# A convolution and an expert network on one core: block 1's convolution one slot later, block 2's input asked for earlier

## The chip, the core and the metric

The kernel runs on one core of a Trainium2 chip. A core has five engines with queues of their own: TensorE (PE in the profile, its weight loads PEld), VectorE (DVE), ScalarE (ACT), GpSimd (POOL) and SyncE (SP), which here only issues transfers. The engines meet at semaphores: an instruction adds to one when it ends, another engine waits until it has reached a value. The metric is the device time of one execution in microseconds (us); smaller is better.

## What is computed

The input x has 8 sequences of 4096 tokens with 192 features each. A causal convolution with 7 taps mixes each token with the six before it; its weights are a softmax over the taps, one set for each of 8 groups of 24 features. Its result goes through W_in (192 x 2048), an exact GELU, and W_out (2048 x 192).

```python
w = softmax(weight)                          # (8 heads, 7 taps)
x_pad = concatenate([zeros(B, 6, D), x], axis=1)
conv[b, s, h, g] = sum_k w[h, k] * x_pad[b, s + k, 24 * h + g]
h = conv.reshape(B * S, 192) @ w_in          # 32768 x 2048
g = 0.5 * h * (1.0 + erf(h / sqrt(2)))
out = g @ w_out                              # 32768 x 192
```

## The kernel before

**Tiling.** The 32768 tokens are two halves of 16384, which sit in the two halves of the 128 partitions. A *block* is a run of tokens taken from both halves at once: blocks 0 to 5 have 256 tokens of each half, all later ones 512 (`WS`, L33). The 192 features are three groups of 64 (`p`), the 2048 hidden features 16 chunks of 128.

**Stages of a block.** SyncE loads x (`load`, L326, four transfers for a block). VectorE transposes it (`trans`, L473) so that features lie on partitions. The convolution follows. From block 2 on, VectorE does it tap by tap (`conv`, L498). For blocks 0 and 1, at the start, TensorE does it, with diagonal matrices of tap weights (`pconv`, L669): first another engine casts the transposed x to bf16 (`cast`, L219; for block 1 that is GpSimd), then TensorE sums the taps into a PSUM bank, and then VectorE (for block 0 also ScalarE) casts the sum to `xc` (`conv_out`, L188). A block has four such sums (`kinds`, L171), called kd 0 to 3; the last two are half as wide. One `pconv` call is a pair of matmuls, one for each half of the tokens.

**Slots and units.** TensorE then runs a block as *slots*. A slot is one call of `mm1` (L706): it multiplies `xc` by some of W_in's columns into one of two PSUM tiles `hp`, and ScalarE takes that tile through GELU into `gT` (L653). With two tiles, slot u waits until the gelu of slot u - 2 has ended (L710). A block of 256 tokens has 8 slots. Between the slots TensorE runs the second product, gT times W_out, of the block before: one call of `mm2` (L749) is a *unit* of two matmuls. A small block has 64 units: two groups of tokens, each with two passes (`ph`) over 16 chunks. In block 0, and in block 1, the units behind the slots are both of block 0's product, since there is none earlier: the first 12 run behind block 0's last slots, the other 52 behind block 1's. The list `ws` (L834) says behind which slots. Block 0's units 0, 4, 8 and 12 each wait for one of W_out's four transfers (`S_WOUT`, L839), and unit 4j of the first group waits for the gelus whose outputs it reads (L765). Unit 16, the first of the second pass, waits for the end of the first pass (L760).

The dictionary `behind` (L704) places block 1's `pconv` pairs behind slots of block 0: `p01` is the 14 pairs of kd 0 and 1, `p2` the 14 half-wide pairs of kd 2 and 3. A convolution pair uses TensorE in tiles of 64 rows by 64 columns. `mm1` uses 64 by 128, but in those of block 0's slots that have convolution pairs behind them and before the next slot it uses twice as many matmuls of 64 by 64 (`fw`, L735).

**W_in in both halves.** Each token half needs W_in on its own partitions. GpSimd loads each column group once, into one half, with six transfers: two counted by `S_WIN[0]` and `S_WIN[1]`, two by `S_WIN[2]`, and two larger ones by `S_WIN[3]` and `S_WIN[4]`. VectorE copies each to the other half (`dup`, L465; six copies, counted by `S_DUPE`). Slots 1, 3, 4 and 6 of block 0 wait for 2, 4, 5 and 6 of these copies (L720).

**Orders written out by hand.** VectorE's order at the start is L545 to L562: among others the copies 3 and 4 (`dup(1, 0)`, `dup(1, 1)`), block 1's last transposition, copy 5, three evictions of block 1 (kd 0 and both halves of kd 1), copy 6 (`dup(2, 1)`), three more evictions, and then block 2's transposition and its convolution. GpSimd's is L424 to L434: the fifth W_in transfer, a wait for the second, the sixth W_in transfer, two W_out transfers, a cast, another cast and a W_out transfer, a third cast and the last W_out transfer. SyncE's is L850 to L861: x of blocks 0 and 1, then a wait, x of block 2, a wait for W_out's last transfer, x of block 3, and from there loads and stores in turn.

Of the kernel before, what the change touches and what calls it, by code (L numbers as in the profile page):

```python
# [11 lines left out]
def bass_lightweight_conv__then__act_gelu_exact_kernel(  # L12
# [54 lines left out]
    NSL = [NF // c for c in NCH]  # L67
# [5 lines left out]
    M0, M1 = 6, NB - 1  # L73

    PHC, MMC, EVC = [0], [0], [0]
    for n in range(NB):
        new = M0 <= n < M1
# [25 lines left out]
    def sem(name):  # L103
        return es.enter_context(nc.semaphore(name))

    def ap(t, off, pat):
        return bass.AP(t, off, pat)

    with es:
# [24 lines left out]
        S_WIN = [sem("S_WIN%d" % i) for i in range(5)]  # L134
        S_WOUT = [sem("S_WOUT%d" % i) for i in range(4)]
# [66 lines left out]
        def wait_pc(e, n, p):  # L202

            if n == 0:
                e.wait_ge(S_PCA, p + 1)
                if p >= 1:
                    e.wait_ge(S_PCE, p)
            else:
                e.wait_ge(S_PCE, len(PV) + (1, 3, 6)[p])
# [23 lines left out]
        def cvd(n):  # L233

            return sum(NCV - 2 * (m in K0) for m in range(n + 1) if m not in PC)
# [58 lines left out]
        def store_half(e, g, h):  # L294
            m = NB - 1
            if h == 0:
                wait_ev(e, m, g)
            else:
                e.wait_ge(S_EVB, g + 1)
            e.dma_start(  # L300
                ap(outt, (h * HALF + OFF[m] + 128 * g) * C, [[C, 128], [1, C]]),
                osb[m % 2][:, (4 * h + g) * C : (4 * h + g + 1) * C],
            ).then_inc(S_OUT[m % 2], 16)
# [22 lines left out]
        def load(e, n, qs=(0, 2, 1, 3), sm=None):  # L326
            mb = WS[n] // 32
            if n >= NX:
                e.wait_ge(S_TR, trd(n - NX))
            for q in qs:  # L330
                off = ((q // 2) * HALF + OFF[n]) * D + DQ * (q % 2)
                dst = [[TB // 32 * DQ, 32], [DQ, mb], [1, DQ]]
                src = [[D, 32], [32 * D, mb], [1, DQ]]
                e.dma_start(
                    ap(xin[n % NX], 32 * q * (TB // 32 * DQ), dst), ap(xt, off, src)
                ).then_inc(sm or S_XIN[n % NX], 16)
# [327 lines left out]
        def _(t):  # L664
# [4 lines left out]
            def pconv(n, kd, k):  # L669

                p, ex, c0, w = kinds(n)[kd]
                if k == KS - 1:
                    t.wait_ge(S_CAST[PC[n]], p + 1)
                    if n == 0:
                        t.wait_ge(S_DG, 1)
                if n == 0 and k == 2:
                    t.wait_ge(S_DGA, 3)
                if k == KS - 2:
                    t.wait_ge(S_HALO, n + 1)
                for hf in range(2):  # L680
                    ho = hf ^ ex
                    r = slice(64 * hf, 64 * hf + 64)
                    d0 = k * 64
                    x0 = p * XB + HF + k + c0
                    ins = t.matmul(  # L685
                        bank(kd, slice(64 * ho, 64 * ho + 64), w),
                        dg[r, d0 : d0 + 64],
                        xTb[PC[n]][r, x0 : x0 + w],
                        start=(k == KS - 1),
                        stop=(k == 0),  # L690
                        tile_position=(64 * hf, 64 * ho),
                    )
                if k == 0:
                    ins.then_inc(S_PC)
# [6 lines left out]

            p01 = [(1, kd, k) for k in taps for kd in (0, 1)]
            p2 = [(1, kd, k) for k in taps for kd in (2, 3)]
            behind = {(0, 2): p01[:8], (0, 3): p01[8:] + p2[:2], (0, 4): p2[2:]}  # L704

            def mm1(n, i):  # L706
                w, c = WS[n], NCH[n]
                u = SL0[n] + i
                if u >= 2:
                    t.wait_ge(S_GELU, u - 1)  # L710
                if i == 0:
                    if n in PC:
                        wait_pc(t, n, NP - 2)
                    else:
                        t.wait_ge(S_CV, cvd(n) - 1)
                if n == 0:
                    for j, k in {0: ((0, 16), (1, 16)), 2: ((2, 32),), 4: ((3, 16),), 6: ((4, 16),)}.get(i, ()):
                        t.wait_ge(S_WIN[j], k)
                    if i in (1, 3, 4, 6):
                        t.wait_ge(S_DUPE, (0, 2, 0, 4, 5, 0, 6)[i])  # L720
                todo = [(cc, p) for cc in range(c) for p in range(NP)]
                head = (n, i) == (0, 0)
                if head:
                    todo.sort(key=lambda q: q[1] == NP - 1)
                for cc, p in todo:
                    if i == 0 and cc == 0 and p == NP - 1:
                        if n in PC:
                            wait_pc(t, n, p)
                        else:
                            t.wait_ge(S_CV, cvd(n))  # L730
                    for hf in range(2):
                        r = slice(64 * hf, 64 * hf + 64)
                        ch = CH[hf][i * c + cc]
                        f0 = FQ * ((ch // 2) ^ hf) + ch % 2
                        fw = 64 if (n == 0 and 3 <= i <= 4) or M0 < n <= M1 else 128  # L735
                        for fo in range(0, 128, fw):
                            f1 = 64 * hf * NP * F + p * F + f0 + 2 * fo
                            o = hf * TB + cc * w
                            ins = t.matmul(  # L739
                                hp[u % 2][fo : fo + fw, o : o + w],  # L740
                                ap(win, f1, [[NP * F, 64], [2, fw]]),
                                xc[n % 2][r, p * TB : p * TB + w],
                                start=(p == 0 and (cc == 0 or not head)),
                                stop=(p == NP - 1 and (cc == c - 1 or not head)),
                                tile_position=(64 * hf, fo),
                            )
                ins.then_inc(S_MM1)
# [68 lines left out]
            SHARE = [3, 3, 3, 3, 4, 3, 3, 3, 3, 4, 3, 3, 3, 3, 2, 2]  # L816

            def units(m):
                if M0 <= m < M1:
                    return [(ps, i) for ps in range(3) for i in range(NF)]  # L820
                return [
                    (g, ph, i) for g in range(NG[m]) for ph in range(2) for i in range(NF)
                ]

            for n in range(NB):
                todo = units(max(n - 1, 0))
                if n < 2:
                    todo = todo[12:] if n else todo[:12]
                for i in range(NSL[n]):
                    mm1(n, i)  # L830
                    for q in behind.get((n, i), []):
                        pconv(*q)
                    new = M0 < n <= M1
                    ws = SHARE if new else [0] * 5 + [1] * 3 if n == 0 else [1] * NSL[n]  # L834
                    a0 = len(todo) * sum(ws[:i]) // sum(ws)
                    a1 = len(todo) * sum(ws[: i + 1]) // sum(ws)
                    for un in todo[a0:a1]:
                        if n < 2 and un[:2] == (0, 0) and un[2] % 4 == 0:
                            t.wait_ge(S_WOUT[un[2] // 4], 16)  # L839
                        (mm2_t if new else mm2)(max(n - 1, 0), *un)  # L840
# [7 lines left out]
        @block.sync  # L848
        def _(sp):
            sp.dma_start(wsb[:, :], ap(wt, 0, [[KS, H], [1, KS]])).then_inc(S_WSB, 16)  # L850
            load(sp, 0, (0, 1))

            sp.wait_ge(S_PRO, 2)
            load(sp, 1)
            sp.wait_ge(S_WOUT[0], 16)
            load(sp, 2)
            sp.wait_ge(S_WOUT[3], 16)
            load(sp, 3)
            for n in range(1, NB):
                if n + 3 < NB:  # L860
                    load(sp, n + 3)  # L861
                store(sp, n - 1)
            for g in range(NG[NB - 1]):
                store_half(sp, g, 0)
            for s in range(2):
                sp.wait_ge(S_OUT[s], OUTS[NB - 1 if (NB - 1) % 2 == s else NB - 2])
# [28 lines left out]
```

## Time and profile before

| what | value |
|---|---|
| median of 4 runs | 680.98 us (680.86 to 681.99) |
| the profiled execution | 680.86 us |
| its span, first to last instruction | 679.1 us |
| granted TensorE clock | 1.000 |
| gelus (L653) | 512, mean 1024 ns |
| mm1 matmuls (L739) | 6072, mean 365 ns |
| block 1's evictions on VectorE begin | 12.97 us |
| VectorE's transposition of block 2 begins | 18.73 us |

Times inside the span are counted from its first instruction. The profiled execution's time is 1.8 us longer than its span, by what lies around the instructions. An engine's busy time is the union of its instructions' times; TensorE's matmuls overlap, so a matmul's duration (0.27 us for 256 columns) is not what it costs, and the distance between starts is. "Idle before" names the semaphore that came last before an instruction.

### The profile page before, as it was taken

What the parts mean: (1) busy time and instruction counts of PE and PEld (TensorE: products, weight loads), DVE (VectorE), ACT (ScalarE), POOL (GpSimd) and SP (SyncE); (2) the same over time, 40 slices, a digit from 0 to 9 for tenths busy, and PEclk for the clock granted to TensorE, in tenths of its full rate; (3) what the DMA queues carried; (4) which work ended last, traced back from release to release, by engine and by line L of the source; (5) the groups of instructions that cost most, each with busy time, mean ns of one, the idle gap of its engine ahead of it and who ended that gap; (6) DMA issues with size and microseconds to landing.
All of it is one profiled execution on the core that took longest, in us unless ns stands there. A gap on an engine that the chain in (4) does not pass through costs nothing.

```text
span 679.1 us, 27122 instructions
## 1 busy us (share of the span) xinstructions
PE 674.2 (99%) x12632; PEld 411.8 (61%) x12632; DVE 527.4 (78%) x609; ACT 537.2 (79%) x550; POOL 32.7 (5%) x56
## 2 busy tenths in 40 slices
PE   8999999999999999999999999999999999999998
PEld 8899655555555555555555555555555555555557
DVE  6889978977779877779777788777797777887511
ACT  7899977787778777787877777877877777778772
POOL 5010000000000000000000000000000000000000
PEclk9999999999999999999999999999999999999999
DMA  9435324224443234442244432244422444310223
GB/s 153 107 95 131 70 61 94 52 50 93 95 96 78 47 68 96 95 96 58 46 90 95 96 76 51 65 96 95 97 57 50 85 96 95 89 37 21 49 49 96
DMA packets 134177, 53.66 MB, mean 79 GB/s; under 512 B 127408, under 2 KB 134064, under 8 KB 134064
## 3 DMA queue, kind: packets, MB, share of 16 engines
q1 hardware_dynamic: 130224, 49.76, 32.6%
q0 software_dynamic: 2720, 1.57, 1.8%
q8 instruction: 99, 1.62, 1.0%
q10 hardware_dynamic: 1120, 0.59, 0.3%
q14 instruction: 14, 0.11, 0.1%
HBM read 28.31 MB, written 25.17 MB: 79 GB/s over the span
## 4 chain that ended last, share of the span: by engine, by line
PE 97%; DMA 1%; POOL 1%; ACT 0%; issue 0%; DVE 0%
PE hp L739 48%; PE ob L800 43%; PE ob L771 5%; PE hp L771 1%; DMA win<-in_moe_w_in_dram 1%; ACT gT L653 0%; POOL wout L404 0%; POOL win L371 0%; DMA wsb<-in_weight_dram 0%; PE ob L685 0%; POOL xTb L226 0%; DVE osb L290 0%
## 5 line engine op out<-in xcount | busy, mean ns | idle before, releaser
L653 ACT ACTIVATE gT<-hp 128x1024 bf16<-128x1024 f32 x512 | 523.3, 1024 | 128.3 <-PE hp L739 124.6
L739 PE MATMUL hp<-xc,win 64*64 64x512 bf16 (+2 forms) x6072 | 418.7, 365 | 0.8 <-ACT gT L653 0.5
L800 PE MATMUL ob<-gT,wout 64*64 64x512 bf16 x5376 | 366.3, 376 | 0.0
L524 DVE SCALAR_TENSOR_TENSOR acc<-xT,wcol,acc 128x1024 f32<-128x1024 f32 (+1 forms) x330 | 295.3, 945 | 3.0 <-ACT acc L626 2.9
L739 PEld LDWEIGHTS hp<-xc,win 64*64 64x64 bf16 (+1 forms) x6072 | 188.5, 106 | 133.6 <-ACT gT L653 0.9
L800 PEld LDWEIGHTS ob<-gT,wout 64*64 64x64 bf16 x5376 | 172.3, 118 | 122.8
L321 DVE STREAM_TRANSPOSE osb<-ob 128x512 f32<-128x512 f32 x84 | 74.4, 888 | 128.9 <-PE ob L800 128.9
L496 DVE STREAM_TRANSPOSE xT<-xin 128x1536 f32<-128x1536 f32 (+2 forms) x39 | 74.9, 1925 | 3.5 <-DMA xin<-in_x_dram 3.4
L524 DVE SCALAR_TENSOR_TENSOR xc<-xT,wcol,acc 128x1024 bf16<-128x1024 f32 (+1 forms) x66 | 60.6, 959 | 0.0
L771 PE MATMUL ob<-wout,gT 64*128 64x192 bf16 x896 | 47.7, 243 | 0.3 <-ACT gT L653 0.2
L422 POOL COPY xT<-xT 128x18 f32<-128x18 f32 x30 | 22.6, 752 | 513.4 <-DVE xT L496 490.7
L771 PEld LDWEIGHTS ob<-wout,gT 64*128 64x128 bf16 x896 | 38.6, 94 | 6.2 <-PE ob L771 0.6
L517 DVE TENSOR_SCALAR acc<-xT,wcol 128x512 f32<-128x512 f32 (+2 forms) x60 | 33.7, 604 | 1.1
L292 ACT ACTIVATE osb<-ob 128x192 f32<-128x192 f32 x2 | 0.7, 332 | 7.1 <-PE ob L771 7.1
L667 PE MATMUL hp<-const-bfloat16-1.0 128*128 128x128 bf16 x48 | 5.3, 313 | 0.8 <-PEq L880 0.8
L771 PE MATMUL hp<-wout,gT 64*128 64x192 bf16 x128 | 5.9, 243 | 0.0
L667 PEld LDWEIGHTS hp<-const-bfloat16-1.0 128*128 128x128 bf16 x48 | 5.0, 149 | 0.8 <-issue 0.8
L290 DVE COPY osb<-ob 128x192 f32<-128x192 f32 x2 | 0.7, 358 | 6.1 <-PE ob L771 6.1
L771 PEld LDWEIGHTS hp<-wout,gT 64*128 64x128 bf16 x128 | 5.3, 94 | 0.0
L626 ACT ACTIVATE acc<-xT,wcol 128x256 f32<-128x256 f32 (+1 forms) x9 | 5.2, 579 | 0.0
L277 ACT ACTIVATE osb<-ob 128x384 f32<-128x384 f32 x10 | 4.9, 485 | 0.0
L685 PE MATMUL ob<-xTb,dg 64*64 64x256 bf16 (+1 forms) x112 | 4.1, 251 | 0.1
(35 smaller groups left out, 30.4 us busy)
## 6 DMA issues: line engine op xcount, KB each, us to landing
out_dram<-osb SPq DMA_DIRECT2D x124, 192.0 KB, 3.2
xin<-in_x_dram SPq DMA_DIRECT2D x116, 192.0 KB, 4.0
xin<-in_x_dram SPq DMA_DIRECT2D x22, 96.0 KB, 2.8
wout<-in_moe_w_out_dram POOLq DMA_DIRECT2D x4, 192.0 KB, 4.8
win<-in_moe_w_in_dram POOLq DMA_DIRECT2D x4, 96.0 KB, 4.8
win<-in_moe_w_in_dram POOLq DMA_DIRECT2D x2, 192.0 KB, 4.4
out_dram<-osb ACTq DMA_DIRECT2D x4, 96.0 KB, 1.9
out_dram<-osb SPq DMA_DIRECT2D x4, 96.0 KB, 2.4
```

The costliest lines, as they stand in the source:

```text
L277: e.activation(out=dst, in_=src, func=AF.Copy).then_inc(S_EVA)
L321: v.transpose(ap(osb[m % 2], j, [[8 * C, 128], [C // 2, TB // 32], [NP, 32]]), bank(ring(m, j)),).then_inc(S_EV)
L422: g.tensor_copy(dst, src).then_inc(S_HALO)
L496: v.transpose(out, src).then_inc(S_TR)
L517: ins = v.tensor_scalar(a, src, wk, None, ALU.mult)
L524: ins = v.scalar_tensor_tensor(dst, src, wk, a, op0=ALU.mult, op1=ALU.add)
L626: a.activation(out=acc[n % 2][:, p * TB : p * TB + w], in_=ap(xT[n % 2], p * XW + HX, [[NP * XW, 128], [1, w]]), func=AF.Copy, scale=wcol[ ...
L653: a.activation(out=ap(gT[n % 2], i * c * 2 * w, dst), in_=ap(hp[u % 2], 0, src), func=AF.Gelu,).then_inc(S_GELU)
L667: t.matmul(hp[1][:, 0:128], one, one)
L739: ins = t.matmul(hp[u % 2][fo : fo + fw, o : o + w], ap(win, f1, [[NP * F, 64], [2, fw]]), xc[n % 2][r, p * TB : p * TB + w], start=(p == ...
L771: ins = t.matmul(bb[sub], gT[m % 2][r, c0 : c0 + 128], wout[r, CH[sub][i] * C : (CH[sub][i] + 1) * C], start=(ph == 0 and k == 0), stop=(p ...
L800: ins = t.matmul(bank(ring(m, j), slice(64 * h, 64 * h + 64), w), ap(wout, 64 * hf * NF * C + CH[h][i] * C + j, [[NF * C, 64], [NP, 64]],) ...
```

## The change

Three things change. Block 1's convolution pairs move from behind slots 2, 3 and 4 to behind slots 3, 4 and 5, in the same three portions, and the tile form of `mm1` follows them. Block 0's units behind its own slots become 8 instead of 12: four each behind slots 6 and 7, none behind slot 5; the other 56 go behind block 1's eight slots, seven each. And SyncE asks for block 2's x when the transfer counted by `S_WIN[3]` (the fifth of W_in, the first of the two larger ones) has landed, where it waited for W_out's first. No instruction is added or removed in sum.

```diff
-            behind = {(0, 2): p01[:8], (0, 3): p01[8:] + p2[:2], (0, 4): p2[2:]}
+            behind = {(0, 3): p01[:8], (0, 4): p01[8:] + p2[:2], (0, 5): p2[2:]}
...
-                        fw = 64 if (n == 0 and 3 <= i <= 4) or M0 < n <= M1 else 128
+                        fw = 64 if (n == 0 and 4 <= i <= 5) or M0 < n <= M1 else 128
...
                 if n < 2:
-                    todo = todo[12:] if n else todo[:12]
+                    todo = todo[8:] if n else todo[:8]
...
-                    ws = SHARE if new else [0] * 5 + [1] * 3 if n == 0 else [1] * NSL[n]
+                    ws = SHARE if new else [0] * 6 + [1] * 2 if n == 0 else [1] * NSL[n]
...
             load(sp, 1)
-            sp.wait_ge(S_WOUT[0], 16)
+            sp.wait_ge(S_WIN[3], 16)
             load(sp, 2)
```

## The prediction

> **What bounds the kernel now.** I read the page's busy times first, then its 40 slices, then the busy times of single stretches.
>
> ```profile
> PE 674.2 (99%) x12632; PEld 411.8 (61%) x12632; DVE 527.4 (78%) x609; ACT 537.2 (79%) x550; POOL 32.7 (5%) x56
> ...
> PE   8999999999999999999999999999999999999998
> ```
> ```profile
> 30.00:650.00 620.00, 620.00 (x11538) 367.52 (x11536) 501.97 (x553) 498.65 (x500) 22.05 (x30) 1.00 0.35 77
> ```
>
> In the stretches each engine has its busy us and, in brackets, its instructions; the last three columns are the clock, the DMA share and GB/s. TensorE (PE) is without a gap from 30 to 650 us. Matmuls overlap in the trace, so I also went through the starts of all matmuls: after 25 us two intervals alone exceed 0.26 us before the tail at 665 us. So the end is set by when TensorE becomes full, and by nothing later. Next, the start on a timeline: TensorE, then ScalarE (ACT), then VectorE (DVE); the columns are start, duration, what, and the idle time before it.
>
> ```profile
> 10.22 0.83 PE L739 MATMUL hp<-xc,win 64*128 64x256 bf16 x12 [0.46 <-ACT gT L653]
> 11.00 1.04 PE L685 MATMUL ob<-xTb,dg 64*64 64x256 bf16 x16
> 11.78 0.92 PE L739 MATMUL hp<-xc,win 64*64 64x256 bf16 x24
> ...
> 15.04 0.83 PE L739 MATMUL hp<-xc,win 64*128 64x256 bf16 x12
> ...
> 18.06 0.91 PE L771 MATMUL ob<-wout,gT 64*128 64x192 bf16 x12 [0.22 <-ACT gT L653]
> ```
> ```profile
> 12.75 6.16 ACT L653 ACTIVATE gT<-hp 128x1024 bf16<-128x1024 f32 x6 [0.63 <-PE hp L739]
> ```
> ```profile
> 12.97 1.33 DVE L200 CAST xc<-ob 128x256 bf16<-128x256 f32 x3 [0.59 <-PE ob L685]
> 14.34 0.56 DVE L469 COPY win<-win 64x1536 bf16<-64x1536 bf16 x1
> 14.81 0.92 DVE L200 CAST xc<-ob 128x128 bf16<-128x128 f32 x3
> 18.73 1.22 DVE L496 STREAM_TRANSPOSE xT<-xin 128x768 f32<-128x768 f32 x1 [3.00 <-DMA xin<-in_x_dram]
> ```
>
> The reader is to see three things. At 11.00 block 1's convolution stands in front of slot 3 and waits for GpSimd's casts, so ScalarE idles 0.63 us. At 17.66 TensorE has issued its last matmul of block 1's slot 0, and stands until 18.06 for the gelu of block 0's slot 7. And VectorE makes the last of its six copies of W_in (14.34) *between* two groups of block 1's evictions; slot 6 starts at 15.04, right behind that copy's end at 14.90. VectorE's 3.00 us before block 2's transposition is long, but is it on the path?
>
> **What the skill says.** Perfetto Trace Analysis, Identifying the Most-Contended Engine: busy time of matmuls is a poor measure of how full TensorE is. The trace agrees: 12 matmuls of a slot show 0.83 us but the next kind starts 0.65 us after the first. I price by starts. DMA: Bandwidth & Descriptors, Issuing engines are not separate DMA queues: transfers from SyncE and GpSimd run on the same 16 engines and interleave. The trace agrees: from 5.0 to 7.5 us GpSimd's queue took 74.0% and SyncE's 50.7% of them together. TensorEngine Tiling (Array Packing), Key Properties: a change of tiling mode drains the array. Here the change from 64*64 to 64*128 ahead of slot 5 cost some 0.09 us (13.915 free, 14.006 started).
>
> **Prices, from starts.** One mm1 slot 0.655 us, in either tile form. One mm2 unit (two matmuls) 0.0825, from eight units in 0.66. Four 64*64 convolution matmuls 0.109 at 256 columns, 0.057 at 128. A gelu is 1.024 and begins 0.87 after its slot's first matmul (15.04 to 15.91, 16.02 to 16.89). A VectorE copy's end to the matmul that needs it: 0.145 (14.892 to 15.038).
>
> **The convolution, one slot later.** Nothing changes up to slot 2 at 10.22, which has issued at 10.88. Slot 3 now follows at once. It needs gelu 1 (ends 11.08) and the fourth W_in copy (two copies, 1.11 us from 10.13, end 11.24), so it starts at 11.38; with the 0.055 lag that the casts show it would be 11.29. It takes the 64*128 form and slot 5 the 64*64 form: 12 matmuls fewer and 12 more at one price, zero. Slot 3 is issued at 12.04. Its gelu can start at 12.25, 0.5 earlier than before: this is the gain. The first eight convolution pairs then cost 0.44 and a mode change, 0.09 (0 to 0.09), to 12.57. The casts, ready at 11.36, are now hidden behind slot 3. Slot 4: 12.57 to 13.22. The other six pairs and two narrow ones: 0.33 + 0.06, to 13.61. Slot 5: to 14.27. Twelve narrow pairs: 0.34, to 14.61. Here TensorE is free.
>
> Slot 6, however, needs the sixth W_in copy, and VectorE does that only after three evictions of block 1, which wait for the first two convolution sums. Their last matmul is issued at 13.44 and ends 0.27 later, so VectorE starts at 13.76 instead of 12.97. Evictions and copy take what they took: 1.92 us from 12.97 to 14.89, so the copy ends at 15.68 and slot 6 starts at 15.82 (15.70 with the short lags). That is 0.78 later than 15.04, and TensorE stands for 1.2 us. VectorE's own slack, the 0.59 us that it idles before the evictions, is no cover: what comes late is the sum that it waits for.
>
> **The eight pairs.** Block 0's product has 64 units. Before, 12 went behind slots 5 to 7 and 6 behind block 1's slot 0: 18 when block 1's slot 1 starts at 18.80. From slot 6 to there: 15.04 to 18.80 is 3.76 = three slots 1.965 + 14 units 1.155 + 0.40 for the gelu of slot 7 + 0.24 for the turn from the 16th unit to the 17th, which waits for the sums of its own bank. After: 4 + 4 + 7 = 15 units. Three slots 1.965 + 15 units 1.24 + 0.08 for the gelu (with the units moved it arrives nearly in time) = 3.28, to 19.10. So 0.30 later, with three units fewer done (0.25) and the turn (0.24) still to come: 0.79 behind. With the short lags: 0.67. I take 0.75.
>
> **Block 2's x.** SyncE's four transfers (384 KB) are issued from 10.7 (the transfer that S_WIN[3] counts lands at 10.63) instead of 13.69. Before, they landed 2.8 to 3.6 us after issue; after, on busier queues, about 16.0. VectorE is free at 15.68 + 0.92 (three narrow evictions) = 16.63 and transposes then, 2.1 us earlier. Worth on TensorE: nothing. Block 2's convolution ended at 27.11, and TensorE, going on from block 0's product without a gap, took up block 2 at 27.34. Its cover is that product's remaining units; if it came 0.3 later it would begin to cost. What is late next is nothing that TensorE waits for.
>
> The price is paid in the DMA engines, on which W_out stands behind:
>
> ```profile
> 12.40:15.00 2.60, 2.60 (x94) 2.37 (x86) 1.93 (x5) 2.17 (x3) 1.11 (x3) 1.00 1.24 176
> 15.00:17.00 2.00, 2.00 (x45) 1.97 (x42) 0.67 (x3) 2.00 (x3) 0.00 (x0) 1.00 1.06 191
> 17.00:18.80 1.80, 1.52 (x30) 1.04 (x26) 0.07 (x1) 1.80 (x2) 0.00 (x0) 1.00 0.45 111
> ```
>
> They are full until 17.4 and then drain. The bytes are the same, so W_out's last transfer, landed at 17.70, moves between 0 and 1.8 us: x's 393 kB, had they all gone first, at the 110 kB per half us that they moved alone from 16.5 to 17.5. I take 18.2. W_out's four parts landed at 13.67, 14.71, 15.65 and 17.70; even 1.8 later, the first three are in time for the units behind slots 6, 7 and block 1's slot 0 (16.47, 17.46, 18.43). Only the fourth, needed at about 18.83, could be late. W_in's last transfer (12.39) would be late only beyond 15.1. SyncE's next load, block 3's, waits for that same fourth landing: some 0.5 later, to land at 23.3 (22.74 before), for a transposition that can't come before 24.9 (27.04 before, less 2.1). Nothing waits.
>
> **Sum.** The profiled execution was 680.86 with a span of 679.10; plus 0.75 makes a span of 679.85 and a time of 681.61. The median of the four runs is 0.12 above the profiled one, so 681.7.
>
> **Rivals.** *The copy isn't late.* If slot 6 could start when TensorE is free, at about 14.65, the gelus would follow each other without a break and end slot 7's at 17.56; block 1's slot 1 would start at 17.95 with 15 units done. Against 18.80 less the 0.49 above, that gains 0.36: 680.6. For it: gelu 3 does start earlier. Against it: VectorE's order is written out by hand, the copy stands behind the evictions, and slot 6 already started on its heels. Chance 0.12; even this lies within 0.1%. To gain over 1.36 us one would have to remove more idle time than the start has.
>
> *W_out's last transfer becomes the wait*, the one that ends slower. Place: the wait before unit 12 of block 0, behind which every matmul of TensorE queues. It decides once the landing comes after 18.7. At the upper bound, 17.70 + 1.8 + 0.14 = 19.64 against 18.83, it costs 0.8 more, together 1.55: 682.5. For it: x's packets go in front of three of W_out's four transfers, on engines with no slack. Against it: the same bytes were through by about 18 before, and interleaving shares rather than puts last. Chance 0.17.
>
> *The earlier x is on the path after all*, through blocks 3 to 5, where VectorE is full until 80 us: then a gain of up to 2 us. Against it stand 620 us without a gap; there is nothing to gain. I give this 0.01, and 0.02 to something slower that I don't see.
>
> **Numbers.** The forecast's chance is 0.68, at 681.3 to 682.1. About 0.2%, 1.36 us, is what a measurement of this kernel can tell from no change. Of the forecast 0.66 fall within it and 0.02 above; of the first rival 0.10 within and 0.02 faster; of the second 0.15 slower and 0.02 within; with the rest: faster 0.03, same 0.78, slower 0.19. The range leaves out the first rival (0.12) and the upper part of the second: 680.8 to 682.6.
>
> **What would show it.** Right: slot 3 starts near 11.4 and its gelu near 12.25; VectorE's evictions start near 13.8 and the copy ends near 15.7; TensorE's gap moves from 17.66 to about 14.6 to 15.8; block 2 is transposed near 16.7; block 1's slot 1 starts near 19.1; the span is 679.7 to 680.0, with nothing different from block 2 on but a shift. Wrong: slot 6 starts before 15.3, or a wait on W_out's landing, or a gap on TensorE after 25 us.

## The result: 0.15% slower, and the profile after

The changed kernel takes 682.15 us (median of 41 runs, 681.39 to 683.25) against 681.00 for the kernel before (61 runs). The ratio is 1.0015, with a 95% interval of 1.0011 to 1.0020: 1.15 us slower, clear of zero, but within the 0.2% that the prediction set as the bound of no change. The forecast was 681.7, in a range of 680.8 to 682.6.

| | before | after |
|---|---|---|
| profiled execution, us | 680.86 | 681.53 |
| its span | 679.1 | 679.7 |
| first gelu of block 0 begins | 9.14 | 8.63 |
| slot 3 / slot 6 begins | 11.78 / 15.04 | 11.13 / 15.61 |
| block 1's slot 1 begins, units done by then | 18.80, 18 | 18.88, 15 |
| block 2's transposition begins | 18.73 | 17.87 |
| W_out's fourth transfer lands | 17.70 | 18.11 |

First the stretches of the profile after, from 30 to 650 us and at the start (columns as above):

```profile
30.00:650.00 620.00, 620.00 (x11540) 369.19 (x11538) 500.94 (x551) 498.47 (x499) 19.08 (x30) 1.00 0.35 77
...
12.40:15.00 2.60, 2.16 (x96) 1.99 (x84) 1.36 (x4) 2.38 (x3) 0.86 (x2) 1.00 1.19 209
15.00:17.00 2.00, 1.39 (x28) 1.42 (x30) 1.24 (x4) 0.81 (x2) 0.00 (x0) 1.00 1.09 207
17.00:18.80 1.80, 1.80 (x41) 1.69 (x39) 0.93 (x1) 1.80 (x3) 0.00 (x0) 1.00 0.08 12
```

TensorE is full from 30 to 650 us in both, so all of the difference arises before. TensorE's busy time now has a hole between 12.4 and 17 us (2.16 of 2.60, 1.39 of 2.00), where it was full, and it is full from 17.0 to 18.8, where it had one. The chain of waits of the profile after, from 9 to 20 us (start, duration, what), says why:

```profile
4.35 4.78 DMA xin<-in_x_dram
9.15 0.93 DVE xT L496 x2
10.11 0.42 DVE win L469
10.56 0.43 DVE win L469
10.99 0.14 issue
11.13 0.83 PE hp L739 x12
...
13.56 0.41 DVE xc L200
14.00 0.42 DVE xc L200
14.43 0.03 issue
14.46 0.43 DVE xc L200
14.91 0.57 DVE win L469
15.47 0.14 issue
15.61 0.83 PE hp L739 x12
```

Before, the same view named GpSimd's casts and ScalarE's gelus:

```profile
10.54 0.83 POOL xTb L226 x2
...
14.88 1.02 ACT gT L653
```

Now the chain runs through VectorE: block 1's x lands, two transpositions, the third and fourth copy of W_in, slot 3, the convolution, three evictions, the sixth copy, slot 6. What the prediction named is all there: the lag of 0.14 from a copy to TensorE twice, and slot 6 behind the copy.

The timeline of the profile after on TensorE, VectorE and ScalarE:

```profile
14.05 0.51 PE L685 MATMUL ob<-xTb,dg 64*64 64x128 bf16 x24
15.61 0.83 PE L739 MATMUL hp<-xc,win 64*128 64x256 bf16 x12 [1.05 <-DVE win L469]
```
```profile
13.54 1.33 DVE L200 CAST xc<-ob 128x256 bf16<-128x256 f32 x3 [1.41 <-PE ob L685]
14.91 0.56 DVE L469 COPY win<-win 64x1536 bf16<-64x1536 bf16 x1
...
17.87 1.23 DVE L496 STREAM_TRANSPOSE xT<-xin 128x768 f32<-128x768 f32 x1 [1.57 <-DMA xin<-in_x_dram]
```
```profile
16.48 2.99 ACT L653 ACTIVATE gT<-hp 128x1024 bf16<-128x1024 f32 x3 [1.19 <-PE hp L739]
```

VectorE idles 1.41 us (0.59 before) for the convolution's sum, and ScalarE 1.19 us for slot 6. From slot 6 to block 1's slot 1 it is 3.27 us, forecast 3.28. By the prediction's own reckoning this execution is 18.88 - 18.80 = 0.08 later, three units short (0.25) and the turn (0.24) ahead of it: 0.57; the spans differ by 0.58. Its first gelu came 0.5 us early, because W_in's first transfer landed early (6.31 instead of 7.07), but that is not what the chain rests on: the chain begins with block 1's x, which landed when it did before (9.13 and 9.15). With 681.53 the execution is one of the fastest of the 41. What makes the median 0.6 slower than that is the question for the experiments.

### The profile page after: what moved, and what is told of

Read it like the earlier page. It is cut to its first block, busy times and chain, and to the rows that moved or that the text cites. A ratio compares the mean times of both kernels' runs of the same rounds, so it can differ in the third digit from the quotient of the medians.

```text
span 679.7 us, 27122 instructions
## 1 busy us (share of the span) xinstructions
PE 673.7 (99%) x12632; PEld 412.8 (61%) x12632; DVE 527.1 (78%) x609; ACT 537.2 (79%) x550; POOL 30.0 (4%) x56
## 4 chain that ended last, share of the span: by engine, by line
PE 98%; DMA 1%; DVE 1%; SPq 0%; issue 0%; ACT 0%; ACTq 0%
PE hp L739 49%; PE ob L800 43%; PE ob L771 6%; PE hp L771 1%; DMA xin<-in_x_dram 1%; DVE win L469 0%; DMA wsb<-in_weight_dram 0%; DVE xc L200 0%; SPq L334 0%; PE ob L685 0%; DVE xT L496 0%; DVE osb L290 0%; ACT wex L589 0%; DVE wrc L448 0%; DVE wmx L442 0%
## 5 line engine op out<-in xcount | busy, mean ns | idle before, releaser
L739 PE MATMUL hp<-xc,win 64*64 64x512 bf16 (+3 forms) x6072 | 418.7, 365 | 2.0 <-DVE win L469 1.6
L422 POOL COPY xT<-xT 128x18 f32<-128x18 f32 x30 | 19.6, 653 | 517.1 <-DVE xT L496 490.1
L200 DVE CAST xc<-ob 64x256 bf16<-64x256 f32 (+3 forms) x8 | 2.8, 355 | 2.1 <-PE ob L685 1.9
```

The source lines that it names most:

```text
L422: g.tensor_copy(dst, src).then_inc(S_HALO)
L739: ins = t.matmul(hp[u % 2][fo : fo + fw, o : o + w], ap(win, f1, [[NP * F, 64], [2, fw]]), xc[n % 2][r, p * TB : p * TB + w], start=(p == ...
```

## Experiments

All were timed in three groups of four, in five rounds beside the kernel before, whose medians in these groups were 681.13, 681.11 and 681.06. A figure such as "+0.51" is a variant's median less the one of its group. The interval of one kernel's ratio is some 0.0007 to either side, 0.5 us: single runs bound an effect, and the pattern over several, with their traces, tells the parts apart. Three variants are also compared with all 62 executions of the changed kernel (41 and 21), which lie 1.09 over before in the median; the intervals of these differences come from resampling the recorded times, each less the median of before in its own group.

**The x request alone (x_only).**

```diff
-            sp.wait_ge(S_WOUT[0], 16)
+            sp.wait_ge(S_WIN[3], 16)
```

> The kernel before with block 2's x asked for after S_WIN[3] and nothing else. If the earlier x costs nothing on TensorE (the prediction's step), the time is that of before within 0.2 us, and VectorE transposes block 2 some 1 to 2 us earlier. If x's 384 KB in front of W_in's last transfer and W_out are what made the changed kernel 0.4 us slower than the sum said, this run is 0.3 to 0.5 us slower, with a later landing of W_in's sixth transfer, of W_out or of block 1's x in the trace.

681.64, +0.51, ratio 1.0008 (1.0002 to 1.0015). The second expectation held. VectorE even transposes block 2 later (19.92), since x landed last at 19.90, between late W_out transfers. The waits of this execution from 10 to 20.3 us:

```profile
PEld ob L771 <- DMA wout<-in_moe_w_out_dram: 1.3, 3, 0.7
PEld hp L739 <- issue: 1.1, 1, 1.1
```

W_out's four parts landed at 15.34, 16.64, 17.89 and 19.48 instead of 13.67 to 17.70, and TensorE waited for them three times. This execution is one of the slower ones (682.41), so its waits show what can happen and do not size the median.

**The convolution alone (conv_only).** The edits of `behind` and `fw`, nothing else.

> The kernel before with block 1's convolution pairs and the tile form moved by one slot; 12 units behind slots 5 to 7 and the x request as before. If the sixth W_in copy, queued behind the evictions, is the whole cost, this run is 0.7 to 0.8 us slower by the sum (1.1 us, if this step was mis-sized), with TensorE idle for about 0.9 us ahead of slot 6. If the fewer units are the cost, it is as fast as before.

681.44, +0.31, ratio 1.0010 (1.0002 to 1.0018); the 13 runs spread from 681.26 to 682.63, with five above 681.6. The profiled execution was the slowest, 682.63: in it the two copies before slot 3 took 1.64 us together, so that slot 3 began at 12.31 only, and W_out's last part landed at 19.78. Slower, as expected, by less than the sum in the median.

**The units alone (units_only).** The edits of `todo` and `ws`, nothing else.

> The kernel before with 8 units behind slots 6 and 7 and 56 behind block 1, the convolution and the x request as before. By the sum it loses nothing and gains nothing (the gelu wait of 0.40 us goes, three units and the turn come later): within 0.2 us of before. If the units are a cost of their own, 0.3 us or more slower.

681.07, -0.04, ratio 1.0001 (0.9993 to 1.0009): the first expectation held, the units cost nothing. In its profile TensorE waits 0.31 us for W_out's fourth transfer, which landed at 18.05, although x was asked for as before.

**Convolution and units, x as before (no_x).** The changed kernel with the x request undone.

> The changed kernel with block 2's x asked for as before (after S_WOUT[0]): the convolution and the units alone. If the earlier x costs the changed kernel nothing, because W_out's fourth transfer at 18.1 us is still ahead of its unit at 18.6, the time is that of the changed kernel, 1.0 to 1.1 us over before. If the earlier x costs 0.5 us here as it did alone, this run is 0.5 us over before.

681.65, +0.54, ratio 1.0008 (1.0000 to 1.0016): the second expectation held. So the convolution and the units together cost some 0.54 (the convolution alone had 0.31; the runs don't tell the two figures apart), and the earlier x adds some 0.45 to 0.6 on top. Its profile (slot 6 at 15.59, block 1's slot 1 at 18.86) gives 0.06 + 0.25 + 0.24 = 0.55 over before.

**The changed kernel again (after_again).**

> The changed kernel once more, for a second profile: in the first one the start was 0.5 us earlier than in the profile of before (first gelu at 8.63 and 9.14). Same time as the changed kernel, some 1.1 us over before. If the start's length varies from run to run with the landing of W_in, slot 6 starts elsewhere than at 15.61, and the distance from slot 3 to slot 6 stays 4.48 us within 0.1.

682.11, +0.98, ratio 1.0014 (1.0008 to 1.0021). Slot 3 began at 11.97, slot 6 at 16.45, 4.48 apart as in the first profile, and block 1's slot 1 at 19.71: 0.91 + 0.49 = 1.40 over before; the spans differ by 1.41. What differs between the two profiles is VectorE's copies before slot 3. The timeline of this execution, VectorE and GpSimd:

```profile
10.20 1.63 DVE L469 COPY win<-win 64x768 bf16<-64x768 bf16 x2
```
```profile
10.12 0.81 POOL L226 CAST xTb<-xT 128x256 bf16<-128x256 f32 x2
```

Two copies take 1.63 us where the first profile has 0.87: the first takes 1.02 instead of 0.42, and starts 0.07 after GpSimd's cast.

**Casts held back (casts_wait, no_x_casts_wait).** To the changed kernel, and to no_x, on GpSimd ahead of the casts:

```diff
+            g.wait_ge(S_DUPE, 4)
             for p in range(NP):
                 cast(g, 1, p)
```

> The changed kernel with GpSimd's three casts of block 1 held until VectorE's fourth W_in copy is done. In five profiles that copy ended at 10.8 to 12.2 us, late where the third copy took 1.0 us instead of 0.42 while GpSimd cast. If this collision is what the sum missed, both copies take 0.42, slot 3 starts at 11.0 to 11.2 in every profile, and the run is 0.3 to 0.5 us faster than the changed kernel. If the collision is only in some profiles and not in the median, there is no gain.

> The convolution and the units alone, x as before, and GpSimd's casts held until the fourth W_in copy. With the casts held the changed kernel gained 0.26 us; if the collision of casts and copies is independent of x, this run gains the same over no_x, 681.3 to 681.5 with slot 3 at 11.0 to 11.2; if the gain came from x, none.

casts_wait: 681.85, +0.74, ratio 1.0012 (1.0005 to 1.0018), 0.24 less than after_again's +0.98, and 0.35 less than the 62 executions (95%: 0.14 to 0.48): near the first expectation's lower end. The copies take what they should:

```profile
10.01 0.87 DVE L470 COPY win<-win 64x768 bf16<-64x768 bf16 x2
```

and slot 3 began at 11.03, but part was given back: W_out's third transfer is queued behind the casts (issued at 11.64, 10.61 in the first profile), and TensorE meets the fourth's landing at 18.89:

```profile
18.93 0.42 PE L772 MATMUL ob<-wout,gT 64*128 64x192 bf16 x6 [0.27 <-DMA wout<-in_moe_w_out_dram]
```

no_x_casts_wait: 681.51, +0.45, 0.09 less than no_x, no gain that these runs resolve. So the collision takes part in the changed kernel's median, by some 0.25 to 0.35; with the old x no gain is resolved.

**No need of W_out's fourth transfer (other_w).** In the changed kernel, units 12 to 15 of block 0 take W_out's chunks 0 to 3, and the wait moves to unit 28; the transfer stays. This kernel leaves out four products that the result needs and has four others in their place, so it only serves to time the wait.

```diff
+                iw = k - 12 if (m, g, ph) == (0, 0, 0) and k >= 12 else k
...
-                        wout[r, CH[sub][i] * C : (CH[sub][i] + 1) * C],
+                        wout[r, CH[sub][iw] * C : (CH[sub][iw] + 1) * C],
```

> The changed kernel with units 12 to 15 of block 0 multiplying W_out's chunks 0 to 3 instead of 12 to 15, so that they need not wait for W_out's fourth transfer; the transfer itself stays, and its wait moves to unit 28. (These four products are replaced by others.) If the 0.45 us by which the changed kernel is above the one with the old x request is a wait for that transfer, the run is 0.3 to 0.5 us faster than the changed kernel, about 681.7. If x costs through something else (W_in's landings, the fetch of instructions), it is as slow as the changed kernel, 682.1.

681.50, +0.44, ratio 1.0008 (1.0000 to 1.0017): as fast as no_x. With that one wait gone and all traffic kept, a cost as large as the earlier x's is gone. Against the 62 executions no_x is 0.55 faster (95%: 0.13 to 0.81) and other_w 0.65 (0.22 to 0.79). Neither profile of the changed kernel caught the wait (landings at 18.11 and 18.17, the unit's turn at 18.56 and 19.40); the profiles of x_only, copy_first and casts_wait did, with landings of 18.89 to 19.48. But the wait isn't the early x's alone: with x asked for as before, the profiles of units_only, conv_only and copy_first_old_x show it too (0.31, 0.23 and 0.20 us). No run takes it away from no_x, so how much of other_w's gain belongs to x stays open.

**The sixth copy first (copy_first, and copy_first_old_x with the x request undone).**

```diff
             dup(2, 0)
-            for j in range(3):
-                conv_out(v, 1, j)
             dup(2, 1)
-            for j in range(3, len(pieces(1))):
+            for j in range(len(pieces(1))):
                 conv_out(v, 1, j)
```

> The changed kernel with VectorE's sixth W_in copy put ahead of block 1's evictions. If that copy behind the evictions is the cost, slot 6 starts at about 14.4 to 14.7 instead of 15.6, and the run is about 1.1 us faster than the changed kernel, 680.6 to 681.0, that is 0 to 0.4 faster than before. If something else holds slot 6 (gelus, W_in's sixth transfer), the gain is under 0.4 us.

> The changed kernel with the sixth W_in copy ahead of the evictions and with x asked for as before. With the copy first alone, slot 6 started at 14.32 but W_out's fourth transfer landed at 18.89 and TensorE waited 0.88 us for it. If x's packets made that landing late, it comes at 17.7 to 18.0 here, and the run is 0.5 to 0.9 us faster than copy_first, 680.7 to 681.2, level with before. If W_out is late by itself, as fast as copy_first.

copy_first: 681.77, +0.64, ratio 1.0014 (1.0006 to 1.0022), far from the full gain. Slot 6 did start early, but TensorE ran into two other waits:

```profile
14.32 0.83 PE L737 MATMUL hp<-xc,win 64*128 64x256 bf16 x12
15.35 0.51 PE L769 MATMUL ob<-wout,gT 64*128 64x192 bf16 x8 [0.19 <-issue]
...
18.93 0.42 PE L769 MATMUL ob<-wout,gT 64*128 64x192 bf16 x6 [0.88 <-DMA wout<-in_moe_w_out_dram]
```

Unit 0 needs the same three evictions (the wait at L756, since the product writes the banks that held the sums), and unit 12 waits for W_out, landed at 18.89. With x asked for as before W_out landed at 18.07 and the time was 680.82, -0.29, ratio 0.9999 (0.9991 to 1.0007): 0.93 less than copy_first's +0.64, as the first expectation had it, and 0.83 less than no_x, from which it differs only in the copy's place. This repairs the change's loss; that it beats the kernel before isn't shown.

**W_out's transfers ahead of the casts too (wout_first, wout_first_old_x).** copy_first and copy_first_old_x with another order on GpSimd:

```diff
-            wout_in(0)
-            wout_in(1)
+            for k in range(4):
+                wout_in(k)
             for p in range(NP):
                 cast(g, 1, p)
-                if p > 0:
-                    wout_in(p + 1)
```

> The changed kernel with two orders mended: the sixth W_in copy ahead of block 1's evictions on VectorE, and on GpSimd all four W_out transfers ahead of the three casts. W_out's last transfer is then issued at about 11 instead of 12.3 to 13.2, and the casts begin after the copies. If W_out's landing and the copy were the two costs, slot 6 starts at 14.3 to 14.5, TensorE does not wait for W_out, and the run is 1.2 to 1.6 us faster than the changed kernel: 680.5 to 680.9. If x's packets hold W_out back wherever it is issued, 681.3 to 681.7.

> The same with x asked for as before. W_out's last transfer lands by 17.3; slot 6 at 14.3 to 14.5; 680.4 to 680.8, that is 0.3 to 0.6 us faster than before, if block 2's convolution (x landing at 18.7) isn't the next wait, at about 27.4; if it is, 680.8 to 681.0.

681.49, +0.43, and 681.32, +0.26, both with a ratio of 1.0008 (1.0000 to 1.0016). For wout_first the second expectation held; wout_first_old_x met neither time. Issued at 10.82 instead of 12.18 (copy_first), W_out's last part still landed at 18.50 instead of 18.89 with the early x, and, issued at 11.08, at 17.57 without: the landing follows what else is on the DMA engines far more than the issue. And three casts in a row now met the fifth W_in copy. VectorE and GpSimd of wout_first:

```profile
11.75 1.99 DVE L467 COPY win<-win 64x1536 bf16<-64x1536 bf16 x2
```
```profile
11.52 1.19 POOL L226 CAST xTb<-xT 128x256 bf16<-128x256 f32 x3
```

The first of these two copies took 1.41 us (0.56 before), slot 4 moved to 13.30, slot 6 to 15.46.

In wout_first_old_x a further wait appears, the one that its second expectation named. Block 2's x landed at 20.12, VectorE's convolution ended at 28.52, and TensorE stood some 0.3 us for it before block 2's first slot at 28.27 and inside it. VectorE's timeline and the wait:

```profile
20.14 1.23 DVE L494 STREAM_TRANSPOSE xT<-xin 128x768 f32<-128x768 f32 x1 [3.08 <-DMA xin<-in_x_dram]
...
27.39 1.13 DVE L522 SCALAR_TENSOR_TENSOR xc<-xT,wcol,acc 128x512 bf16<-128x512 f32 x2
```
```profile
PEld hp L735 <- DVE xc L522: 0.2, 1, 0.2
```

The profile of copy_first_old_x has the same wait (x landed at 19.51, the convolution ended at 27.91). In these two executions the later request for x has a cost, as the prediction said it would once block 2's convolution came some 0.3 us later.

## Why the prediction was right, and where its size was off

The measured 682.15 lies inside the range and just above the forecast's own 681.3 to 682.1. That it came so close is in part luck, since two errors of size offset each other: the sum is some 0.2 too large for an execution without collisions (0.57, the profile after), and the 0.6 from there to the median's 1.15 was not in it: the collision of copies with GpSimd's work and the wait for W_out.

- *The end is set by the start.* Right for the change. The start of block 1's slot 1 less 18.80, plus 0.49 for the units and the turn, gives the span over before within 0.02 us: 0.57 for 0.58, 1.40 for 1.41, 0.55 for 0.54 (after, after_again, no_x). The clear exceptions are copy_first_old_x (0.07 for 0.34) and wout_first_old_x (0.67 for 0.95), where TensorE stands again for block 2's convolution.
- *The convolution: slot 6 waits for the sixth copy.* The mechanism was right: the copy put ahead of the evictions takes the cost away (copy_first_old_x). The 0.75 was somewhat large: no_x has 0.55 in its profile and 0.54 in the median, though its interval, 0 to 1.1 us, holds 0.75 too. Slot 3 was put at 11.38, from the copies' 1.11 us in the profile before; undisturbed they take 0.87, and slot 3 starts at 11.1. The 1.11 already held a little of a collision with GpSimd, up to 1.64 in other executions. The Trainium skill (SBUF — State Buffer, section SBUF: two separate sides) says that VectorE and GpSimd share a port pair, and that of a GpSimd instruction and a VectorE one in a mode that uses the pair, the one that starts first holds it for its whole instruction. The traces fit that for the casts: where a cast began 0.02 to 0.23 us ahead of it, a copy took 0.75 (copy_first_old_x) and 1.02 (after_again) instead of 0.42, and 1.41 instead of 0.56 (wout_first, three casts), and where the copy began 0.04 ahead, it was the cast that took 0.77 instead of 0.40 (after). A cast does not explain the first copy of the profile before, which took 0.66 though it began 0.35 ahead of the first cast; but GpSimd was issuing a W_out transfer then. GpSimd before, then VectorE and GpSimd of wout_first:

```profile
9.78 0.76 POOL L404 DMA_DIRECT2D wout<-in_moe_w_out_dram  x1
10.48 0.88 POOL L226 CAST xTb<-xT 128x256 bf16<-128x256 f32 x2
```
```profile
9.96 1.20 DVE L467 COPY win<-win 64x768 bf16<-64x768 bf16 x2
```
```profile
8.72 2.90 POOL L404 DMA_DIRECT2D wout<-in_moe_w_out_dram  x4
```

In wout_first no cast ran yet, and the two copies took 0.59 and 0.57 beside such issues. So the issue of a transfer is the likelier cause of the 0.66; no run isolates it.

Before, slot 3 followed the convolution and the casts, and this scatter was nearly covered; now slot 3 stands directly behind the copies.

- *The eight pairs.* Fewer units done and a gelu that is no longer waited for should cancel. Right, -0.04 alone.
- *The earlier x is worth nothing on TensorE, and W_out stays in time.* The first half is right for the changed kernel, whose block 2 was ready at 26.25 for a slot at 27.99; the second is the term of the sum that was mis-sized. W_out's fourth landing was put at 18.2, needed at 18.83 (at 18.56 in the profile after). In the traces with the early x it fell between 18.1 and 19.5, in those without between 17.2 and 18.4 and once at 19.78, and taking its wait away (other_w) took off as much as x had added, 0.45 to 0.6 us. What the prediction held as the rival that ends slower takes part in the median, at less than its 0.8. By the medians: 0.54 for the convolution and the units and 0.45 to 0.6 for x make 1.0 to 1.15, of which the forecast had 0.75. That it is this wait in most executions rests on other_w alone; the two profiles of the changed kernel don't show it.
- *VectorE earlier by 2.1 us*: it was 0.9 in the profile, since x landed at 17.84 and not at 16.0. The shortfall costs nothing.
- *The first rival*, that the copy isn't late, fell; copy_first shows that behind it stood the wait of unit 0 for the same evictions, which the prediction had not seen.
- *Two intervals between matmul starts above 0.26 us, after 25 us.* The trace has none from 25 to 665 us; the two begin at 24.47 and 665.25. That TensorE is full in between stands.

## What to carry to other kernels

When work is moved behind another step, look at what else stands in that step's engine order behind its result: here a copy that had no need of the convolution waited for it only because it was queued after its evictions. A transfer asked for earlier on full DMA engines can delay the ones that it passes, as W_out's fourth here, and is worth that only if its own receiver is on the path. Price a step from an undisturbed execution, and give the step that takes its cover away the scatter of that price.

## What the runs showed of the hardware that was not expected

GpSimd's casts can hold up VectorE's bf16 copies in SBUF: with casts that began 0.06 to 0.07 us ahead, 0.42 us became 1.02 and 1.03 (after_again, conv_only), while a copy that began 0.36 us behind a cast kept its 0.42 (after). And in x_only TensorE started no matmul from 13.27 to 14.38, in the middle of a slot and without a wait that the profile shows. In the packet records a 16 KB transfer of the instruction queue took 2.53 us there (10.53 to 13.06), against 0.9 to 1.7 in the starts of the other profiles. That the traffic delayed TensorE's instructions is a guess from this one case; it wasn't tried.
